# A list schedule that looks at all engines at once, with other tile counts and due times, in a chain of three kernels on one core

## The chip, the cores and the metric

The kernel runs on one core of a Trainium2 chip. The metric is the device time of one execution in microseconds, the median of a few runs. A profile of one execution shows what each engine did: TensorE (PE, with its weight loads as PEld), VectorE (DVE), ScalarE (ACT), GpSimd (POOL), and the queue of SyncE (SP), which issues all DMAs.

## The reference: what is computed

Three blocks follow one another, for a batch of 4:

```python
x  = attention(q_l, k_l, v_l, q_g, k_g, v_g)   # 8 heads of 64; 512 local positions with a
                                               # window of 32 to each side, 32 global positions
x  = moe(x, w_gate, wq, wk, wv, wo)            # 576 positions, 4 experts of causal attention (64 wide),
                                               # the best 2 of 4 by the gate, summed by their weights
h  = relu(x @ w_in)                            # 512 -> 1024
c  = conv over 3 neighbouring positions of h
y  = (h * sigmoid(c)) @ w_out                  # 1024 -> 512
```

`w_in`, `conv_w` and `w_out` arrive as 64-bit floats, and the kernel makes 32-bit floats of them (the "decode"). Every matrix product of the last two blocks is made of three products of high and low halves (`gh`/`gl`, `wuh`/`wul` and so on), each at one pass.

## The kernel before

All work of the program is recorded first and then put in order by a list schedule (`Recorder.schedule`). Each recorded piece has a due time, a number written by hand (`due(...)`, from the constants at the head: `PERIOD`, `A_AT`, `B_AT`, `FOLD`, `WOUT`, ...), a planned cost, and the tiles that it uses. The schedule walks through planned time and gives each engine that is free the ready piece with the lowest due time. A piece that begins a new tile is passed over while all buffers of that name are in use. The outcome is a fixed order of instructions on each engine; on the chip every engine takes its own in that order and waits where data or a buffer is not there yet. All engine calls are made on one line (308), so the rows of the profile are told apart by tile names.

The work of the program, by the functions that record it:

- `fold_gen`: 16 pieces of `w_in`, each loaded (256 KB), decoded by six DVE instructions and one of ACT, split into halves (`gl`; the low one by POOL) and multiplied with `wo` on PE into `wfh`/`wfl`. 16 pieces of `w_out` follow in `wout_gen`: the same decode, then `wuh` by ACT and `wul` by POOL. Columns 0 to 255 of `w_out` come first, then columns 256 to 511.
- `phase_a(b)`: the local and global attention in four chunks of two heads (`a0` to `a3` stand for the four batches below, `c0` to `c3` for the four chunks; tiles `raw`, `Pa`, `Pg`, `PA`, `vr`, `xh`, `xl`).
- `phase_b(b)`: the projections with `wqk` and `wv`, then 8 items of causal attention (scores `s<-kh,qh`, softmax in `w`, transposes, product with `vB`, result in `oh`/`ol`), and one for the last 32 rows.
- `phase_c(b)`: for two halves z of the positions, 8 times `s0` (PE `s<-oh,wfh`, ACT `hb` and `cv`), `s1` (two DVE `cv<-hb,cw,cv`, ACT), `s2` (DVE `cv<-cv,hb`, ACT `gh`, DVE `gl`), and then `project` (PE `s<-gh,wuh`, `s<-gl,wuh`, `s<-gh,wul`, in four column blocks m; m 0 and 1 need columns 0 to 255 of `w_out`, m 2 and 3 the rest).

The tile names that the change touches: `w2` (five buffers of 544 columns, for raw 64-bit weights, softmax rows and other weights alike), `d0`/`d1` (two buffers each, the decode's work tiles; `d` in the rows), `hb`/`cv` (three each). The decode of one piece on DVE is:

```python
dve.tensor_scalar(ai, up, 3, 0x3FFFFFF8, op0=ALU.logical_shift_left, op1=ALU.bitwise_and)
dve.scalar_tensor_tensor(di, up, -0x40000000, ai, op0=ALU.bitwise_and, op1=ALU.bitwise_or)
dve.tensor_scalar(ai, di, -0x800000, None, op0=ALU.bitwise_and)
dve.scalar_tensor_tensor(a, lo.bitcast(U32), 2.0 ** -52, a, op0=ALU.mult, op1=ALU.mult)
dve.tensor_tensor(d, d, a, op=ALU.add)
act.activation(a, up.bitcast(F32), AF.Abs)
dve.scalar_tensor_tensor(dst, a, GUARD, d, op0=ALU.is_ge, op1=ALU.mult)
```

Of the kernel before, what the change touches and what calls it, by code (L numbers as in the profile page):

```python
# [19 lines left out]
S = SL + SG  # L20
# [11 lines left out]
FIRST = [min(KEYS.index(n - 1), KEYS.index(n + 1) - 3) for n in range(NG_)]  # L32


PERIOD, A_AT, A_STEP, LOAD_AHEAD = 60.0, 0.0, 10.0, 20.0
B_AT, LAST, ITEMS, ITEM_STEP = 30.0, 34.0, 14.0, 2.5
C_AT, C_HALF, C_PROJ = 75.0, 25.0, 12.0
FOLD, FOLD_STEP, WOUT, WOUT_STEP = 30.0, 2.5, 75.0, 2.5


def local_mask():
# [110 lines left out]
class Recorder:  # L152
# [72 lines left out]
    def schedule(self):  # L225

        import heapq
        waits, after = {}, {}
        for n in self.nodes:
            waits[n] = len(n.deps)  # L230
            for d in n.deps:
                after.setdefault(d, []).append(n)
        used, left = {}, {}
        for n in self.nodes:
            for t in n.tiles:
                left[t] = left.get(t, 0) + 1
        last = {}
        ready = {}
        at = {}
        engines = []  # L240
        for n in self.nodes:
            if n.eng not in engines:
                engines.append(n.eng)
        free = {e: 0.0 for e in engines}
        ready = {e: [] for e in engines}
        for n in self.nodes:
            at[n] = 0.0
            if not waits[n]:
                ready[n.eng].append(n)
        times = [0.0]  # L250
        order, dma, now, back = [], 0.0, 0.0, []
        while len(order) < len(self.nodes):
            if not times:
                stuck = [(n.eng.name, n.due, n.calls[0][0], [t.name for t in n.new]) for e in engines for n in ready[e]]
                raise RuntimeError(f"no order: {stuck[:20]}")
            now = heapq.heappop(times)
            while times and times[0] <= now + 1e-9:
                heapq.heappop(times)
            for t0, t in [x for x in back if x[0] <= now + 1e-9]:
                used[t.name] -= 1  # L260
            back = [x for x in back if x[0] > now + 1e-9]
            lacking = set()
            for e in engines:
                if free[e] > now + 1e-9:
                    continue
                for n in sorted(ready[e], key=lambda n: (n.due, n.seq)):
                    if at[n] > now + 1e-9:
                        continue
                    need = {}
                    for t in n.new:  # L270
                        need[t.name] = need.get(t.name, 0) + 1
                    short = [k for k, c in need.items() if used.get(k, 0) + c > [t.bufs for t in n.new if t.name == k][0]]
                    if short or lacking & set(need):
                        lacking |= set(short)
                        continue
                    ready[e].remove(n)
                    for k, c in need.items():
                        used[k] = used.get(k, 0) + c
                    n.start = now
                    if e.name == "SP":  # L280
                        free[e] = now + 0.45
                        dma = max(dma, now + 0.5) + n.cost
                        n.end = dma + 1.6
                    else:
                        free[e] = n.end = now + n.cost
                    order.append(n)
                    heapq.heappush(times, free[e])
                    for m in after.get(n, ()):
                        at[m] = max(at[m], n.end + (0.02 if m.eng is e else n.lag))
                        waits[m] -= 1  # L290
                        if not waits[m]:
                            ready[m.eng].append(m)
                            heapq.heappush(times, at[m])
                    for t in n.tiles:
                        left[t] -= 1
                        last[t] = max(last.get(t, 0.0), n.end)
                        if not left[t]:
                            back.append((last[t] + 0.1, t))
                            heapq.heappush(times, last[t] + 0.1)
                    break  # L300
        return order

    def emit(self, tc):
# [75 lines left out]
def body(ctx, tc, kq, vA, w_gate, wqk, wv, woT, w_in, conv_w, w_out, cmask, out):  # L379
    nc = tc.nc  # L380
    NB = kq.shape[0]
    rec = Recorder()
    pe, act = rec.engine("PE", nc.tensor, cost_pe), rec.engine("ACT", nc.scalar, cost_act)
    dve, pool = rec.engine("DVE", nc.vector, cost_dve), rec.engine("POOL", nc.gpsimd, cost_pool)
# [5 lines left out]
    def T(shape, dt, name, bufs=1):  # L390
        return rec.tile(sb, shape, dt, name, bufs)
# [4 lines left out]
    def PS(*shape):  # L396
        return rec.tile(ps, [128] + list(shape), F32, "s", 5)
# [1 line left out]
    def PO(*shape):  # L399
        return rec.tile(ps, [128] + list(shape), F32, "t", 3)  # L400

    NW = 5

    def W2(dt=F32, n=512):
        w = T([128, S], F32, "w2", NW)[:, :n]
        return w if dt == F32 else w.bitcast(dt)

    def W1(name, dt=F32):
        w = T([128, 274], F32, name, 3)
        return w if dt == F32 else w.bitcast(dt)  # L410

    NG = 8
# [5 lines left out]
    def scale_pool(dst, src, s):  # L418
        pool.tensor_scalar(dst, src, s, 1.0, op0=ALU.mult, op1=ALU.mult)
# [240 lines left out]

    def consts_a():
        due(-15)
        w = W2()[:, :512]
        sp.dma_start(w, cmask[:, :512])
        dve.tensor_copy(lmask, w)

# [22 lines left out]
    def phase_b(b):  # L689
# [63 lines left out]
        for e in range(4):  # L753
            r0, p = 64 * (e % 2), e // 2
            for d, a in ((ql, qh), (qll, qlo)):
                act.activation(d[r0:r0 + 64, p, 32 * e:32 * e + 32], a[r0:r0 + 64, p, 512:544].bitcast(F32), AF.Copy)
        PL = W2(n=S)
        ms = T([128, 8], F32, "ms_last")
        tl = []
        for z in range(2):  # L760
            t = PS(512)
            n = 0
            if z == 0:
                rec.claim(PL)
            with rec.group():
              for p in range(2):
                for a, k in ((ql, kh), (ql, kl), (qll, kh)):
                    pe.matmul(t[:, :272], a[:, p], k[:, p, 272 * z:272 * z + 272], start=(n == 0),
                              stop=(n == 5 and z == 0))
                    n += 1  # L770
              if z:
                pe.matmul(t[:, 240:272], identb, last_mask, start=False, stop=True)
            dve.tensor_reduce(ms[:, z:z + 1], t[:, :272], axis=AX.X, op=ALU.max, negate=True)
            tl.append(t)
        dve.tensor_tensor(ms[:, 2:3], ms[:, 0:1], ms[:, 1:2], op=ALU.min)
        for z in range(2):
            act.activation(PL[:, 272 * z:272 * z + 272], tl[z][:, :272], AF.Exp, bias=ms[:, 2:3],
                           accum_out=ms[:, 4 + z:5 + z])
# [3 lines left out]
        scale_pool(PL, PL, ms[:, 7:8])  # L782
        PLT = T([128, 5, 128], F32, "PLT")
        t = PO(4, 128)
        rec.claim(PLT)
        with rec.group():
          for j in range(4):
            pe.transpose(t[:, j, :], PL[:, 128 * j:128 * j + 128], ident)
        act.activation(PLT[:, :4], t, AF.Copy)
        t = PO(4, 128)  # L790
        pe.transpose(t[:32, 0, :], PL[:, 512:544], ident)
# [223 lines left out]
```

## Time and profile before

| | us |
|---|---|
| median of 3 runs | 538.84 |
| lowest to highest | 538.46 to 539.15 |
| the profiled execution, its own time | 538.88 |
| its span, first to last instruction | 536.7 |
| PE busy | 480.3 |
| DVE busy | 372.1 |
| ACT busy | 316.6 |
| POOL busy | 127.5 |

The span is what the engines' rows cover; 2.2 us of the execution's own time lie outside of it. Busy PE time holds stretches in which the granted TensorE clock was at the lower of its two levels, so it is not the work at full clock. Shares over the whole span hide that the first third and the rest have different limits, so the rows further down are by stretches.

### The profile page before, as it was taken

What the parts mean: (1) busy time and instruction counts of PE and PEld (TensorE: products, weight loads), DVE (VectorE), ACT (ScalarE), POOL (GpSimd) and SP (SyncE); (2) the same over time, 40 slices, a digit from 0 to 9 for tenths busy, and PEclk for the clock granted to TensorE, in tenths of its full rate; (3) what the DMA queues carried; (4) which work ended last, traced back from release to release, by engine and by line L of the source; (5) the groups of instructions that cost most, each with busy time, mean ns of one, the idle gap of its engine ahead of it and who ended that gap; (6) DMA issues with size and microseconds to landing.
All of it is one profiled execution on the core that took longest, in us unless ns stands there. A gap on an engine that the chain in (4) does not pass through costs nothing.

```text
span 536.7 us, 14628 instructions
## 1 busy us (share of the span) xinstructions
PE 480.3 (89%) x5688; PEld 408.2 (76%) x5688; DVE 372.1 (69%) x1059; ACT 316.6 (59%) x1048; POOL 127.5 (24%) x222
## 2 busy tenths in 40 slices
PE   3777899977659999999999999999999999988997
PEld 1545689745445699997888799978888999767886
DVE  1789899989995846687567855556585646665760
ACT  1656574465555647765368875453796755536771
POOL 2234323244335330013322120131401201230000
PEclk9778999967666999999999999999999999999998
DMA  8475562435530100011015040000321000000001
GB/s 308 147 249 193 177 204 81 134 135 190 191 131 1 54 1 1 22 62 51 22 67 195 24 161 4 2 22 22 132 81 62 24 2 0 23 22 1 22 21 43
DMA packets 19045, 44.06 MB, mean 82 GB/s; under 512 B 2848, under 2 KB 8096, under 8 KB 18976
## 3 DMA queue, kind: packets, MB, share of 16 engines
q1 hardware_dynamic: 18976, 43.12, 23.8%
q8 instruction: 45, 0.74, 0.6%
q14 instruction: 24, 0.20, 0.1%
HBM read 38.66 MB, written 4.46 MB: 80 GB/s over the span
## 4 chain that ended last, share of the span: by engine, by line
PE 55%; DVE 11%; ACT 5%; issue 2%; POOL 0%; DVEq 0%; ACTq 0%; POOLq 0%
PE s L308 41%; PE t L308 13%; DVE cv L308 5%; DVE d L308 1%; ACT cv L308 1%; DVE gl L308 1%; ACT hb L308 1%; DVE PT L308 1%; DVE ml L308 1%; DVE stB L308 1%; ACT Pa L308 1%; ACT gh L308 0%; ACT PA L308 0%; ACT w L308 0%; POOL w L308 0%
## 5 line engine op out<-in xcount | busy, mean ns | idle before, releaser
L308 PE MATMUL s<-gh,wuh 128*128 128x272 f32 x256 | 79.1, 309 | 2.7 <-ACT gh L308 2.7
L308 DVE SCALAR_TENSOR_TENSOR cv<-hb,cw,cv 128x272 f32<-128x272 f32 x128 | 65.6, 524 | 22.3 <-ACT cv L308 19.3
L308 PE MATMUL s<-gl,wuh 128*128 128x272 f32 x256 | 75.3, 294 | 2.9 <-DVE gl L308 2.5
L308 PE MATMUL s<-gh,wul 128*128 128x272 f32 x256 | 74.5, 291 | 0.0
L308 POOL TENSOR_SCALAR w<-w,stB,gate 128x128 f32<-128x128 f32 (+3 forms) x64 | 40.3, 639 | 132.5 <-DVE stB L308 49.5
L308 PE MATMUL s<-raw 64*32 64x128 f32 (+2 forms) x1088 | 46.9, 329 | 13.3 <-DMA raw<-in_kq_dram 6.9
L308 PEld LDWEIGHTS s<-gh,wuh 128*128 128x128 f32 x256 | 49.0, 191 | 6.4 <-ACT gh L308 3.8
L308 PEld LDWEIGHTS s<-gl,wuh 128*128 128x128 f32 x256 | 49.0, 191 | 5.0 <-DVE gl L308 5.0
L308 POOL TENSOR_TENSOR Pa<-Pa,ml 128x512 f32<-128x512 f32 x32 | 36.2, 1147 | 67.0 <-DVE ml L308 33.7
L308 PEld LDWEIGHTS s<-gh,wul 128*128 128x128 f32 x256 | 48.9, 191 | 0.0
L308 PEld LDWEIGHTS s<-raw 64*32 64x32 f32 (+1 forms) x1088 | 24.9, 125 | 30.8 <-issue 12.7
L308 ACT ACTIVATE w<-s,stB 128x128 f32<-128x128 f32 (+3 forms) x64 | 33.3, 525 | 24.7 <-DVE stB L308 21.1
L308 ACT ACTIVATE Pa<-s,ml 128x128 f32<-128x128 f32 x128 | 45.1, 374 | 0.7 <-DVE ml L308 0.7
L308 PE MATMUL s<-oh,wfh 128*128 128x274 f32 x128 | 39.9, 312 | 0.2 <-ACT hb L308 0.2
L308 DVE TENSOR_REDUCE stB<-s 128x1 f32<-128x128 f32 (+3 forms) x64 | 29.4, 484 | 12.6 <-PE s L308 12.5
L308 DVE COPY PT<-t 128x128 f32<-128x128 f32 (+3 forms) x64 | 29.9, 486 | 11.5 <-PE t L308 11.0
L308 PE MATMUL s<-ol,wfh 128*128 128x274 f32 x128 | 37.8, 295 | 0.0
L308 PE MATMUL s<-oh,wfl 128*128 128x274 f32 x128 | 37.7, 294 | 0.0
L308 PE MATMUL s<-xh,wqkh 128*128 128x272 f32 x128 | 37.7, 294 | 0.0
L308 PE MATMUL s<-xh,wqkl 128*128 128x272 f32 x128 | 36.9, 289 | 0.0
L308 PE MATMUL s<-xl,wqkh 128*128 128x272 f32 x128 | 36.8, 288 | 0.0
L308 ACT ACTIVATE cv<-cv 128x272 f32<-128x272 f32 x64 | 27.5, 430 | 15.3 <-DVE cv L308 14.4
(140 smaller groups left out, 1301.6 us busy)
## 6 DMA issues: line engine op xcount, KB each, us to landing
vr<-in_vA_dram SPq DMA_DIRECT2D x32, 512.0 KB, 5.3
raw<-in_kq_dram SPq DMA_DIRECT2D x16, 672.0 KB, 4.1
out_dram<-y SPq DMA_DIRECT2D x32, 136.0 KB, 1.8
w<-in_w_in_dram SPq DMA_DIRECT2D x16, 256.0 KB, 3.4
w<-in_w_out_dram SPq DMA_DIRECT2D x16, 256.0 KB, 2.6
w<-in_wqk_dram SPq DMA_DIRECT2D x4, 256.0 KB, 6.6
w<-in_wv_dram SPq DMA_DIRECT2D x4, 128.0 KB, 2.0
w<-in_woT_dram SPq DMA_DIRECT2D x2, 256.0 KB, 2.8
```

Source lines behind the costliest of these rows:

```text
L308: getattr(n.eng.nc, method)(*map(real, args), **{k: real(v) for k, v in kw.items()})
```

## The change

`schedule` is rewritten: at each step of planned time the ready pieces of all engines are looked at in one list, by due time. The first piece in the list of each engine that is busy (`AHEAD = 1`) reserves its new tiles; when a tile name is short for a piece, all buffers of that name count as taken for the pieces behind it. Before, the engines were gone through one after the other, and only engines that were free.

The due times change a little (`FOLD` from 30 to 20.5 most). Raw 64-bit weights get two tiles of their own, `w64`; `w2` has four buffers of 512 columns; `hb` and `cv` have four buffers each and serve the decode too, in place of `d0`/`d1`. The decode's add goes from DVE to POOL. The score rows for the last 32 positions are cut at 512 and 32 columns in place of 272 and 272.

```diff
+AHEAD = 1
-PERIOD, A_AT, A_STEP, LOAD_AHEAD = 60.0, 0.0, 10.0, 20.0
-B_AT, LAST, ITEMS, ITEM_STEP = 30.0, 34.0, 14.0, 2.5
...
+FOLD, FOLD_STEP, WOUT, WOUT_STEP = 20.5, 2.5, 75.0, 2.5
...
-            lacking = set()
-            for e in engines:
-                if free[e] > now + 1e-9:
+            held, seen = dict(used), {}
+            for n in sorted((n for e in engines for n in ready[e] if at[n] <= now + 1e-9), key=lambda n: (n.due, n.seq)):
+                e = n.eng
+                busy = free[e] > now + 1e-9
+                if busy and seen.get(e, 0) >= AHEAD:
                     continue
...
+                short = [k for k, ts in need.items() if held.get(k, 0) + len(ts) > ts[0].bufs]
+                for k in short:
+                    held[k] = need[k][0].bufs
+                if short:
+                    continue
+                for k, ts in need.items():
+                    held[k] = held.get(k, 0) + len(ts)
+                if busy:
+                    seen[e] = seen.get(e, 0) + 1
+                    continue
...
-    NW = 5
-
-    def W2(dt=F32, n=512):
-        w = T([128, S], F32, "w2", NW)[:, :n]
-        return w if dt == F32 else w.bitcast(dt)
+    def W2():
+        return T([128, 512], F32, "w2", 4)
 
     def W1(name, dt=F32):
-        w = T([128, 274], F32, name, 3)
+        w = T([128, 274], F32, name, 4)
...
-        a, d = T([128, 256], F32, "d0", 2)[:, :w], T([128, 256], F32, "d1", 2)[:, :w]
+        a, d = W1("hb")[:, :w], W1("cv")[:, :w]
...
-        dve.tensor_tensor(d, d, a, op=ALU.add)
+        pool.tensor_tensor(d, d, a, op=ALU.add)
...
-        raw = W2(I32)
+        raw = T([128, 512], F32, "w64", 2).bitcast(I32)
...
-        PL = W2(n=S)
+        PL = W2(), T([128, 32], F32, "PL")
+        keys = slice(0, 512), slice(512, 544)
```

What stands where on the engines moves as follows. On PE, right behind the last product of `fold_gen` (`s<-gl,oh`) and one piece of scores, the order before goes on with the attention chunks of batch 1 (`raw`, `Pg`, `Pa`, `PGT`):

```order
L308 MATMUL s<-raw 32x128 x32
L308 MATMUL s<-raw 64x64
L308 MATMUL t<-ident,Pg 128x64 x6
L308 MATMUL s<-raw 64x480
L308 MATMUL s<-raw 64x64
L308 MATMUL t<-PGT,vr 64x32 x12
L308 MATMUL t<-ident,Pa 128x128 x8
```

In the order of the change the last product of `fold_gen` is followed by the items of batch 0's causal attention (`PT,vB`, `w`, `kh,qh`):

```order
L314 MATMUL s<-gl,ol 128x256
L314 MATMUL t<-PT,vB 64x128 x2
L314 MATMUL t<-ident,w_1522 128x128
L314 MATMUL t<-ident,w_1527 128x128
L314 MATMUL t<-PT,vB 64x128 x2
L314 MATMUL s<-kh,qh 128x256 x2
L314 MATMUL s<-kl,qh 128x256 x2
L314 MATMUL s<-kh,qlo 128x256 x2
```

So the causal attention of batch 0 stands ahead of three chunks of batch 1 and most of one of batch 2, behind which it stood before. `phase_c(0)` follows it, mixed with those chunks.

On DVE, near the last pieces of `w_out` (raw tiles `w_2030` to `w_2105`), the order before has decode steps (`d`) and steps of the local attention (`ml`) alone:

```order
L308 TENSOR_SCALAR d_2257<-d_2260 128x256
L308 TENSOR_TENSOR d_2254<-d_2254,d_2227 128x256
L308 SCALAR_TENSOR_TENSOR d_2257<-w_2085,d_2257 128x256
L308 TENSOR_SCALAR ml<-ml 128x4
L308 SCALAR_TENSOR_TENSOR d_2254<-d_2227,d_2254 128x256
L308 TENSOR_TENSOR d_2260<-d_2260,d_2257 128x256
L308 TENSOR_SCALAR d_2286<-w_2105 128x256
L308 TENSOR_REDUCE ml<-s 128x4
```

In the change, pieces of `w_out` (raw tiles `w_2354`, `w_2434`) stand between the convolution steps of `phase_c(0)` (128x272), with both in `hb` and `cv`:

```order
L314 TENSOR_TENSOR gl<-cv,gh 128x272
L314 SCALAR_TENSOR_TENSOR cv<-cv,hb 128x272
L314 SCALAR_TENSOR_TENSOR cv<-hb,cw,cv 128x272
L314 TENSOR_SCALAR hb<-w_2354 128x256
L314 TENSOR_TENSOR gl<-cv,gh 128x272
L314 SCALAR_TENSOR_TENSOR cv<-cv,hb 128x272
L314 SCALAR_TENSOR_TENSOR cv<-w_2354,hb 128x256
L314 TENSOR_SCALAR hb<-w_2434 128x256
L314 TENSOR_SCALAR hb<-cv 128x256
L314 TENSOR_TENSOR gl<-cv,gh 128x272
```

The decode no longer stands with chunks alone: the items and half of `phase_c(0)` have moved in beside it. The decode's add is gone from DVE. On POOL, at the first pieces of `w_out`, the change has it as `cv<-cv,hb`, between the scalings of the softmax rows (`w`) and the low halves (`wul`):

```order
L314 TENSOR_SCALAR w_1522<-w_1522,stB,gate 128x128
L314 TENSOR_SCALAR w_1527<-w_1527,stB,gate 128x128
L314 TENSOR_TENSOR cv<-cv,hb 128x256 x2
L314 TENSOR_TENSOR wul<-cv,wuh 128x256 x2
L314 TENSOR_TENSOR cv<-cv,hb 128x256
L314 TENSOR_SCALAR w_1657<-w_1657,stB,gate 128x256
```

Before, this place on POOL held `wul` and the scalings of the local attention alone; there are 32 such adds of 128x256 in the program. From the first `s0` of batch 1's `phase_c` on, both orders have the same pieces still to do, but for one score piece of 64 rows, which the change has done by then. Between the end of `fold_gen` and the last product of `project` for z = 0 of batch 0, the change has on PE what the order before has there, less these, which come later: four of the 13 groups of batch 1's projections, batch 1's first score piece, and in batch 2 the last transposes of chunk 0 and the first part of chunk 1.

## Rows read from the trace of the kernel before

**Rows 1.** The page's first part: busy time, share and instructions of each engine.

```profile
PE 480.3 (89%) x5688; PEld 408.2 (76%) x5688; DVE 372.1 (69%) x1059; ACT 316.6 (59%) x1048; POOL 127.5 (24%) x222
```

**Rows 2.** Busy time by stretches; last: granted clock, DMA share, GB/s.

```profile
27.00:104.90 77.90, 67.77 (x944) 56.52 (x942) 72.20 (x200) 46.47 (x166) 26.30 (x28) 0.93 0.52 169
104.90:156.80 51.90, 35.02 (x638) 24.81 (x634) 48.05 (x124) 28.63 (x106) 20.22 (x23) 0.70 0.53 181
156.80:203.40 46.60, 42.08 (x410) 31.81 (x409) 29.90 (x93) 26.20 (x105) 17.77 (x28) 0.86 0.05 16
203.40:233.40 30.00, 30.00 (x245) 29.67 (x244) 23.24 (x73) 21.75 (x59) 2.00 (x13) 1.00 0.03 11
233.40:281.50 48.10, 47.03 (x607) 39.67 (x606) 31.45 (x94) 27.70 (x94) 11.72 (x20) 1.00 0.16 56
281.50:384.70 103.20, 101.98 (x1225) 89.12 (x1223) 64.84 (x197) 64.25 (x215) 20.92 (x42) 1.00 0.22 73
384.70:486.80 102.10, 98.81 (x1133) 87.12 (x1132) 62.80 (x184) 61.77 (x198) 20.31 (x44) 1.00 0.08 28
486.80:536.70 49.90, 42.75 (x292) 40.01 (x289) 27.51 (x65) 28.57 (x73) 1.28 (x13) 0.93 0.07 23
```

**Rows 3.** PE in order of time: start, duration; end of a projection, and batch 1's phase_c.

```profile
233.22 0.29 PE L308 MATMUL s<-gh,wul 128*128 128x272 f32 x1
233.35 0.29 PE L308 MATMUL s<-oh,wfh 128*128 128x274 f32 x1
...
281.51 0.40 PE L308 MATMUL s<-oh,wfh 128*128 128x274 f32 x1
```

**Rows 4.** DVE groups by shape: busy us, mean ns, then idle before.

```profile
L308 DVE TENSOR_SCALAR d<-w 128x256 int32<-128x256 int32 x32 | 19.5, 618 | 1.8 <-DMA w<-in_w_in_dram 1.6
L308 DVE SCALAR_TENSOR_TENSOR d<-w,d 128x256 int32<-128x256 int32 x32 | 18.5, 579 | 0.6 <-POOL gl L308 0.3
L308 DVE SCALAR_TENSOR_TENSOR d<-d,d 128x256 f32<-128x256 f32 x32 | 16.6, 519 | 1.5 <-ACT d L308 1.1
L308 DVE SCALAR_TENSOR_TENSOR d<-w,d 128x256 f32<-128x256 uint32 x32 | 14.7, 459 | 0.6
L308 DVE TENSOR_TENSOR d<-d,d 128x256 f32<-128x256 f32 x32 | 14.2, 443 | 0.2
L308 DVE TENSOR_SCALAR d<-d 128x256 int32<-128x256 int32 x32 | 12.2, 382 | 0.3
```

**Rows 5.** DVE in order of time near 156 to 160 us: start, duration.

```profile
155.59 0.41 DVE L308 TENSOR_TENSOR d<-d,d 128x256 f32<-128x256 f32 x1
155.92 0.41 DVE L308 SCALAR_TENSOR_TENSOR d<-w,d 128x256 f32<-128x256 uint32 x1
...
156.55 0.42 DVE L308 SCALAR_TENSOR_TENSOR d<-d,d 128x256 f32<-128x256 f32 x1
...
157.23 0.29 DVE L308 TENSOR_SCALAR d<-w 128x256 int32<-128x256 int32 x1
...
158.43 0.41 DVE L308 SCALAR_TENSOR_TENSOR d<-w,d 128x256 int32<-128x256 int32 x1
...
158.88 0.29 DVE L308 TENSOR_SCALAR d<-d 128x256 int32<-128x256 int32 x1
...
159.67 0.83 DVE L308 TENSOR_TENSOR d<-d,d 128x256 f32<-128x256 f32 x1
```

**Rows 6.** POOL in order of time, the same stretch.

```profile
157.51 0.72 POOL L308 TENSOR_TENSOR wul<-d,wuh 128x256 fp32r<-128x256 f32 x1 [3.40 <-ACT wuh L308]
159.25 0.97 POOL L308 TENSOR_TENSOR wul<-d,wuh 128x256 fp32r<-128x256 f32 x1 [1.02 <-ACT wuh L308]
```

**Rows 7.** POOL groups over the whole span.

```profile
L308 POOL TENSOR_SCALAR w<-w,stB,gate 128x128 f32<-128x128 f32 (+3 forms) x64 | 40.3, 639 | 132.5 <-DVE stB L308 49.5 <-ACT cv L308 21.5 <-ACT PGT L308 21.0
...
L308 POOL TENSOR_TENSOR gl<-d,gl 128x256 fp32r<-128x256 f32 x16 | 12.7, 803 | 27.6 <-ACT gl L308 20.1 <-ACT gate L308 5.7 <-PE s L308 1.6
L308 POOL TENSOR_TENSOR wul<-d,wuh 128x256 fp32r<-128x256 f32 x16 | 12.3, 775 | 22.0 <-ACT wuh L308 22.0
```

**Rows 8.** Waits, over the whole span: us in total, times, longest.

```profile
DVE stB L308 <- PE s L308: 12.5, 20, 1.3
DVE PT L308 <- PE t L308: 11.0, 22, 1.6
```

More of the change, by code (lines that the diff above doesn't have):

```diff
@@ L32 @@
 FIRST = [min(KEYS.index(n - 1), KEYS.index(n + 1) - 3) for n in range(NG_)]
-PERIOD, A_AT, A_STEP, LOAD_AHEAD = 60.0, 0.0, 10.0, 20.0
-B_AT, LAST, ITEMS, ITEM_STEP = 30.0, 34.0, 14.0, 2.5
-C_AT, C_HALF, C_PROJ = 75.0, 25.0, 12.0
-FOLD, FOLD_STEP, WOUT, WOUT_STEP = 30.0, 2.5, 75.0, 2.5
+AHEAD = 1
+PERIOD, A_AT, A_STEP, LOAD_AHEAD = 60.0, -1.0, 10.0, 20.0
+B_AT, LAST, ITEMS, ITEM_STEP = 30.0, 35.0, 13.5, 2.4
+C_AT, C_HALF, C_PROJ = 75.0, 23.0, 11.0
+FOLD, FOLD_STEP, WOUT, WOUT_STEP = 20.5, 2.5, 75.0, 2.5
 def local_mask():
@@ L261, in schedule @@
             back = [x for x in back if x[0] > now + 1e-9]
-            lacking = set()
-            for e in engines:
-                if free[e] > now + 1e-9:
-                    continue
[L266 to L300, printed above, removed]
@@ new lines, in schedule @@
+            held, seen = dict(used), {}
[3 more added lines that the diff above has]
+                if busy and seen.get(e, 0) >= AHEAD:
+                    continue
+                need = {}
+                for t in n.new:
+                    need.setdefault(t.name, []).append(t)
+                short = [k for k, ts in need.items() if held.get(k, 0) + len(ts) > ts[0].bufs]
[8 more added lines that the diff above has]
+                    continue
+                for k, ts in need.items():
+                    used[k] = used.get(k, 0) + len(ts)
+                ready[e].remove(n)
+                n.start = now
+                if e.name == "SP":
+                    free[e] = now + 0.45
+                    dma = max(dma, now + 0.5) + n.cost
+                    n.end = dma + 1.6
+                else:
+                    free[e] = n.end = now + n.cost
+                order.append(n)
+                heapq.heappush(times, free[e])
+                for m in after.get(n, ()):
+                    at[m] = max(at[m], n.end + (0.02 if m.eng is e else n.lag))
+                    waits[m] -= 1
+                    if not waits[m]:
+                        ready[m.eng].append(m)
+                        heapq.heappush(times, at[m])
+                for t in n.tiles:
+                    left[t] -= 1
+                    last[t] = max(last.get(t, 0.0), n.end)
+                    if not left[t]:
+                        back.append((last[t] + 0.1, t))
+                        heapq.heappush(times, last[t] + 0.1)
@@ L662, in consts_a @@
         due(-15)
-        w = W2()[:, :512]
+        w = W2()
         sp.dma_start(w, cmask[:, :512])
@@ L760, in phase_b @@
         for z in range(2):
-            t = PS(512)
+            w = keys[z].stop - keys[z].start
+            t = PS(512)[:, :w]
             n = 0
-            if z == 0:
-                rec.claim(PL)
+            rec.claim(PL[z])
             with rec.group():
[L766 to L773, printed above, removed]
+                for p in range(2):
+                    for a, k in ((ql, kh), (ql, kl), (qll, kh)):
+                        pe.matmul(t, a[:, p], k[:, p, keys[z]], start=(n == 0), stop=(n == 5 and z == 0))
+                        n += 1
+                if z:
+                    pe.matmul(t, identb, last_mask, start=False, stop=True)
+            dve.tensor_reduce(ms[:, z:z + 1], t, axis=AX.X, op=ALU.max, negate=True)
             tl.append(t)
@@ L776, in phase_b @@
         for z in range(2):
-            act.activation(PL[:, 272 * z:272 * z + 272], tl[z][:, :272], AF.Exp, bias=ms[:, 2:3],
-                           accum_out=ms[:, 4 + z:5 + z])
+            act.activation(PL[z], tl[z], AF.Exp, bias=ms[:, 2:3], accum_out=ms[:, 4 + z:5 + z])
         dve.tensor_scalar(ms[:, 6:7], ms[:, 4:5], ms[:, 5:6], EPS, op0=ALU.add, op1=ALU.add)
@@ L781, in phase_b @@
         dve.tensor_tensor(ms[:, 7:8], ms[:, 6:7], glast, op=ALU.mult)
-        scale_pool(PL, PL, ms[:, 7:8])
+        for z in range(2):
+            scale_pool(PL[z], PL[z], ms[:, 7:8])
         PLT = T([128, 5, 128], F32, "PLT")
@@ L786, in phase_b @@
         with rec.group():
-          for j in range(4):
-            pe.transpose(t[:, j, :], PL[:, 128 * j:128 * j + 128], ident)
+            for j in range(4):
+                pe.transpose(t[:, j, :], PL[0][:, 128 * j:128 * j + 128], ident)
         act.activation(PLT[:, :4], t, AF.Copy)
         t = PO(4, 128)
-        pe.transpose(t[:32, 0, :], PL[:, 512:544], ident)
+        pe.transpose(t[:32, 0, :], PL[1], ident)
         act.activation(PLT[:32, 4], t[:32, 0], AF.Copy)
```

## The prediction

> **What bounds the kernel now.** I read the page's busy line first, then busy time by stretches cut where the program passes from one part to the next, then what DVE's decode steps take alone and beside POOL.
>
> The page says PE 89%, DVE 69% [rows 1], which reads like a PE-bound kernel. The stretches say otherwise [rows 2]. From 27.0 to 104.9 us (the fold and the chunks of batch 0) DVE is busy 72.20 of 77.9 us and from 104.9 to 156.8 (the w_out decode beside the chunks of batch 1) 48.05 of 51.9: 93% both times. PE is busy 35.02 of 51.9 in the second, at a mean granted clock of 0.70, so much of its busy time is the lower level. There DVE is the limit. From 203.4 on it turns: PE is busy 30.00 of 30.0, 47.03 of 48.1, 101.98 of 103.2 and 98.81 of 102.1 at clock 1.00, while DVE falls to 63% and 62% in the last two. Between, from 156.8 to 203.4, batch 0's causal attention runs with DVE busy 29.90 of 46.6. So DVE-heavy work and PE-heavy work stand one behind the other in the first half, and the second half is PE's. In the last stretch, 486.8 to 536.7, PE is busy 42.75 of 49.9: nothing is left to fill the waits of the last convolution.
>
> **The change, part by part.** Call F the end of the fold on PE, 104.9 us, and X the end of the projection for z = 0 in batch 0, 233.4 us [rows 3]. Call C the first product of batch 1's phase_c, 281.5 us [rows 3]. The order shows that the change has between F and X almost the work of before, but with causal attention and phase_c of batch 0 set beside the w_out decode, not behind it. So the question is how fast DVE can get through F to X, and whether PE keeps up.
>
> *DVE's work from F to X.* Before it is 48.05 + 29.90 + 23.24 = 101.2 us of busy time [rows 2], spread over 128.5 us. The change takes 16 of the 32 adds out of it: half of 14.2 us, 7.1 [rows 4]. The steps that go with the PE pieces moved behind X (reductions of one chunk, copies of a projection, of a kind that takes 0.16 to 0.7 us each) and with two first items moved ahead of F I put at 4 us, an estimate.
>
> *What the add costs on POOL, and DVE by it.* The rows have no such add on POOL; the nearest are its subtractions of the same shape, 803 and 775 ns [rows 7], so I take 0.79 us, 25 us for 32. POOL is busy 24% [rows 1], so it has the room. But DVE slows beside it. Alone the six decode steps on DVE take 0.29 + 0.41 + 0.29 + 0.41 + 0.41 + 0.42 = 2.23 us [rows 5]; their means over the program add up to 0.618 + 0.579 + 0.382 + 0.459 + 0.443 + 0.519 = 3.00 [rows 4]. One can be seen at it: the add at 159.67 takes 0.83 us, not 0.41 [rows 5], and a POOL subtraction runs from 159.25 to 160.22 [rows 6]. The excess is 0.77 us a piece, 24.6 us for 32, while POOL was busy 26.30 + 20.22 us [rows 2] and 0.72 + 0.97 up to the last piece [rows 6], 48.2 together: 0.51 us of DVE for a us of POOL. So an add saves DVE 0.44 us and costs it 0.79 x 0.51 = 0.40. The move to GpSimd is worth nothing to DVE, within 0.1 us a piece. From F to X that is +6.4 us for 16, and before F 16 adds leave (-7.1) and come back (+6.4): F is at 104.2, within 4 us. POOL's softmax scalings of the items (40.3 / 4 = 10.1 us a batch [rows 7]) now fall on a fuller DVE; I add 2 us, with 0 and 5 as bounds.
>
> The Trainium skill, in "SBUF — State Buffer", section "Who interferes with whom", says that a DVE instruction with two SBUF inputs, or in a two-port mode, and a GpSimd instruction that reads SBUF hold one shared pair of ports, and that the later one stands until the earlier has ended. The trace agrees with the direction (0.83 for 0.41 us), and by the mean it is half of that price. By the rule at its full length each add would cost DVE 0.79 us and save 0.44, so this part of the change would lose, and the sum below would come to 539 in place of 526.
>
> *X and C.* 101.2 - 7.1 - 4 + 6.4 + 2 = 98.5 us of DVE. At the 93% that DVE reaches where it is the limit [rows 2], that takes 105.9 us, so X comes at 104.2 + 105.9 = 210.1 in place of 233.4. From X to C PE was full, 48.1 us; now the pieces moved behind X are added. The four groups have 12 products each at 0.13 us from one start to the next [rows 3], 6.2 us; the rest I put at 60% of a chunk, with a chunk at (35.02 x 0.70) / 3.7 = 6.6 us of full clock [rows 2], 4.0 us. So C comes at 210.1 + 48.1 + 10.2 = 268.4, 13.1 us earlier.
>
> *Does PE keep up?* Its work from F to X at full clock is at most 35.02 x 0.70 + 42.08 x 0.86 + 30.0 = 90.7 us [rows 2], less 10: 81 in 106 us, a load of 0.76. In the first stretch a load of 67.77 x 0.93 / 77.9 = 0.81 went with a clock of 0.93 [rows 2]; at that clock 81 us of work take 87. It does, unless the clock stays low.
>
> *Behind C.* PE has 4.5 us of idle time from 281.5 to 486.8 and 7.2 from there to the end [rows 2]. The fourth buffer of hb and cv lets the last convolution run one step further ahead; I take 1 us of the 7.2, bounds 0 and 3. The two tiles for raw weights, four w2 in place of five (an item holds two, so two items are under way with either), and the cut at 512 and 32 columns I cost at nothing: their cover is PE's full stretches; if the rows of PE show gaps there, up to 4 us are lost. One POOL scaling becomes two, at most 0.4 us a batch, seen at the end of the last batch alone.
>
> The sum: 538.9 (the profiled execution, which is the median within 0.1) - 13.1 - 1 = 524.8; with 1 us for the last scaling and what the joints between the parts lose, 526.
>
> **The rivals.** *DVE waits inside the items (slower).* DVE takes its instructions as written, and each item has four places where it stands for another engine. From 156.8 to 203.4 it was idle 16.7 us with the items at hand [rows 2], and the waits for PE alone are 12.5 and 11.0 us over four batches [rows 8]. If all 16.7 come along into the decode stretch, X is at 227, C at 285.5, the end at 543. It decides from 13 us on. For it: PE's clock there may be low, so scores come late. Against: decode steps stand between the steps of an item in the order, and DVE, slowed by POOL, tends to be the late one.
>
> *The ports take their full price.* Each POOL us then costs DVE one, not 0.51: 0.39 us more for an add, 12.5 for 32, and about 1 us for the scalings. F moves by 6, X by 13: 539, no change. Against: the means of 32 pieces [rows 4], from which 0.51 comes. This is the rule of the Trainium skill, "SBUF — State Buffer", section "Who interferes with whom", with each add at its full length.
>
> *PE's clock stays low.* At 0.70, as in 104.9 to 156.8 [rows 2], 81 us of work take 116, X is at 220, the end at 535. For it: that stretch has decode and chunks, and half of the new stretch has too. Against: the load is 0.76, not 35.02 x 0.70 / 51.9 = 0.47.
>
> *Better.* DVE runs without gaps, 98.5 us in place of 105.9 (-7.4), and the fold, whose first loads now stand earlier in the SP queue, ends some us sooner: 513 to 518.
>
> **How the numbers follow.** My forecast as told, 519 to 533: 0.50. Better: 0.13. Low clock: 0.11. Full port price: 0.10. Waits in the items: 0.16. The likeliest gives 526. The range goes down to 513 and up to 541, which leaves out part of the slowest rival and a little below the best. A run tells 0.2% (1.1 us) from no change. Faster: 0.50 + 0.13 + 0.11 and 0.03 of the full price, 0.77. Same: 0.06. Slower: 0.17.
>
> **What would show it.** DVE busy 90% or more from the fold's end to the last piece of w_out, which then comes near 205 us; the end of batch 0's z = 0 projection at 210, and batch 1's first phase_c product near 269. From there to the end 254 us as before, within 3. Five decode steps on DVE with means that add up to 2.9 to 3.0 us without the add, if POOL costs what I take; 2.6, the five of today, if the adds cost nothing more. POOL adds near 0.79 us. PE's clock above 0.85 from 105 to 210. It would be wrong if DVE shows waits for PE, ACT or POOL of more than 13 us in that stretch, if F itself came later than 110, or if PE lost more than 5 us behind C because of the other tile counts.

## The result and the profile after

| | before | after |
|---|---|---|
| median, us | 538.79 (538.46 to 539.15, 4 runs) | 515.58 (512.06 to 516.68, 4 runs) |
| profiled execution, us (span) | 538.88 (536.7) | 516.68 (514.9) |

The ratio is 0.9558, with a 95% interval of 0.9512 to 0.9604: 23 us faster. The forecast was 526.0, 13 us faster, so the direction was right, the time was within the range, and the gain was nearly twice what was told.

The page's busy line of after answers to [rows 1]:

```profile
PE 468.6 (91%) x5688; PEld 400.2 (78%) x5688; DVE 359.1 (70%) x1026; ACT 313.5 (61%) x1048; POOL 155.5 (30%) x259
```

PE does as many matmuls, 5,688, in 11.7 us less busy time: less of it falls on the lower clock (the mean granted clock of the span is 0.936 before and 0.970 after). The other 10.1 of the 21.8 us by which the span is shorter were idle time of PE. DVE lost 33 instructions and 13.0 us, POOL gained 28.0.

Busy time by stretches of after, with the columns of [rows 2]. The cuts are the fold's end (109.9), the start of batch 0's phase_c (152.6), the end of its projection z = 0 (208.6), and the first product of phase_c of batches 1, 2 and 3:

```profile
27.00:109.90 82.90, 70.31 (x989) 59.19 (x979) 65.87 (x181) 46.80 (x171) 38.37 (x47) 0.92 0.47 151
109.90:152.60 42.70, 35.66 (x489) 24.39 (x489) 40.10 (x117) 27.14 (x102) 27.29 (x34) 0.96 0.30 103
152.60:208.60 56.00, 51.77 (x621) 46.67 (x620) 47.13 (x120) 41.70 (x137) 23.15 (x39) 0.94 0.30 102
208.60:268.40 59.80, 58.91 (x775) 49.19 (x773) 38.05 (x129) 35.60 (x124) 15.02 (x23) 1.00 0.23 74
268.40:369.90 101.50, 100.88 (x1221) 88.98 (x1220) 65.14 (x194) 64.02 (x216) 21.33 (x45) 1.00 0.19 62
369.90:471.00 101.10, 98.96 (x1133) 87.04 (x1132) 62.44 (x184) 59.29 (x194) 19.60 (x45) 1.00 0.09 30
471.00:514.90 43.90, 39.18 (x292) 36.91 (x289) 26.14 (x65) 27.71 (x73) 1.19 (x12) 0.99 0.08 27
```

Beside [rows 2], the last three stretches took 103.2, 102.1 and 49.9 us before; now they take 101.5, 101.1 and 43.9. The two cuts that the prediction calls X and C stand in PE's rows in order of time (start, duration), which answer to [rows 3]:

```profile
208.26 0.29 PE L314 MATMUL s<-gh,wul 128*128 128x272 f32 x1
...
268.37 0.39 PE L314 MATMUL s<-oh,wfh 128*128 128x274 f32 x1
```

X came at 208.6 (forecast 210.1, before 233.5) and C at 268.4 (forecast 268.4, before 281.5). So 13.1 us come from ahead of C, as told, and 8.7 from behind it, where 1 was told. All that lies ahead of C, before and after, in the columns of [rows 2]:

```profile
0.00:281.50 281.50, 236.79 (x3046) 191.95 (x3046) 216.99 (x613) 161.98 (x564) 84.96 (x124) 0.89 0.34 115
0.00:268.40 268.40, 229.62 (x3049) 187.27 (x3049) 205.33 (x583) 162.43 (x566) 113.42 (x159) 0.94 0.38 125
```

Of the 13.1 us, 7.2 are busy time of PE, at a mean granted clock of 0.94 and not 0.89, and 5.9 are its idle time.

The decode's DVE steps by shape, answering to [rows 4], and below them the add, which is now on POOL (there with one short form more):

```profile
L314 DVE SCALAR_TENSOR_TENSOR cv<-w,hb 128x256 int32<-128x256 int32 x32 | 19.2, 600 | 0.3
L314 DVE SCALAR_TENSOR_TENSOR cv<-hb,cv 128x256 f32<-128x256 f32 x32 | 17.0, 534 | 2.8 <-ACT hb L314 2.8
L314 DVE SCALAR_TENSOR_TENSOR hb<-w,hb 128x256 f32<-128x256 uint32 x32 | 16.1, 504 | 0.5
L314 DVE TENSOR_SCALAR hb<-w 128x256 int32<-128x256 int32 x32 | 13.6, 424 | 4.7 <-DMA w<-in_w_in_dram 4.5 <-DMA w<-in_w_out_dram 0.2
L314 DVE TENSOR_SCALAR hb<-cv 128x256 int32<-128x256 int32 x32 | 12.3, 384 | 0.3
...
L314 POOL TENSOR_TENSOR cv<-cv,hb 128x256 f32<-128x256 f32 (+1 forms) x33 | 26.0, 788 | 48.8 <-DVE hb L314 39.3 <-ACT Pa L314 4.8 <-DVE ml L314 2.8
```

The five means add up to 2.45 us; the same five were 2.56 before [rows 4], and 2.9 to 3.0 were told. The add takes 0.79 us on POOL, as told.

### The profile page after: what moved, and what is told of

Its sections match the earlier page's. It is cut to its first block, busy times and chain, and to the rows that moved or that the text cites. A ratio compares the mean times of both kernels' runs of the same rounds, so it can differ in the third digit from the quotient of the medians.

```text
span 514.9 us, 14575 instructions
## 1 busy us (share of the span) xinstructions
PE 468.6 (91%) x5688; PEld 400.2 (78%) x5688; DVE 359.1 (70%) x1026; ACT 313.5 (61%) x1048; POOL 155.5 (30%) x259
## 4 chain that ended last, share of the span: by engine, by line
PE 68%; DVE 16%; DMA 6%; ACT 5%; POOL 3%; issue 2%; SPq 0%; POOLq 0%; ACTq 0%; DVEq 0%
PE s L314 52%; PE t L314 16%; DVE cv L314 7%; DMA raw<-in_kq_dram 3%; DMA w<-in_w_in_dram 2%; DVE hb L314 2%; DVE gl L314 1%; DVE mg L314 1%; DVE stB L314 1%; DVE ml L314 1%; POOL w L314 1%; ACT hb L314 1%; POOL Pa L314 1%; ACT Pa L314 1%; DVE wqkl L314 1%
## 5 line engine op out<-in xcount | busy, mean ns | idle before, releaser
L314 POOL TENSOR_SCALAR w<-w,stB,gate 128x128 f32<-128x128 f32 (+3 forms) x64 | 41.5, 659 | 116.0 <-DVE gate L314 51.2
L314 POOL TENSOR_TENSOR Pa<-Pa,ml 128x512 f32<-128x512 f32 x32 | 37.3, 1183 | 46.4 <-DVE ml L314 24.8
L314 PE MATMUL s<-raw 64*32 64x128 f32 (+2 forms) x1088 | 43.7, 308 | 7.8 <-DMA raw<-in_kq_dram 6.7
L314 POOL TENSOR_TENSOR cv<-cv,hb 128x256 f32<-128x256 f32 (+1 forms) x33 | 26.0, 788 | 48.8 <-DVE hb L314 39.3
L314 PEld LDWEIGHTS s<-raw 64*32 64x32 f32 (+1 forms) x1088 | 22.9, 117 | 20.7 <-issue 11.1
```

The costliest lines, as they stand in the source:

```text
L314: getattr(n.eng.nc, method)(*map(real, args), **{k: real(v) for k, v in kw.items()})
```

## The experiments

All of them in one table. Ratios are to the kernel before on the same chip. X, C and the last convolution are read from PE's rows in order of time: "C to end" is from C to the end of the span, "last conv." from the first product of batch 3's phase_c to the end of the span, both from times rounded to a tenth. An early C is not all gain, because the orders differ in what stands ahead of it: in *tiles alone* and in *after, old table* 5.2 us less of PE's work stands there than in after, in *after, add on DVE* 6.6 us less, and in *after, three hb and cv* 4 to 5 us less (estimates, by the mean PE time of each kind of piece).

| kernel | median, us | ratio (95%) | X | C | C to end | last conv. |
|---|---|---|---|---|---|---|
| before | 538.8 | 1 | 233.5 | 281.5 | 255.2 | 49.9 |
| after | 515.58 | 0.9558 (0.9512 to 0.9604) | 208.6 | 268.4 | 246.5 | 43.9 |
| tiles alone | 518.52 | 0.9629 (0.9589 to 0.9669) | 200.1 | 259.4 | 256.3 | 43.9 |
| work tiles alone | 528.94 | 0.9822 (0.9782 to 0.9861) | 232.1 | 281.2 | 245.7 | 43.8 |
| schedule alone | 540.36 | 1.0028 (1.0004 to 1.0052) | 235.7 | 283.7 | 254.6 | 48.5 |
| table alone | 550.79 | 1.0228 (1.0200 to 1.0256) | 238.7 | 287.5 | 261.8 | 52.5 |
| add alone | 545.89 | 1.0142 (1.0085 to 1.0199) | 242.6 | 289.8 | 251.9 | 48.4 |
| add alone, order kept | 540.00 | 1.0029 (1.0006 to 1.0051) | 234.0 | 282.2 | 256.8 | 51.5 |
| after, three hb and cv | 529.74 | 0.9835 (0.9801 to 0.9869) | 201.1 | 266.0 | 263.6 | 50.0 |
| after, old schedule | 512.97 | 0.9534 (0.9506 to 0.9563) | 206.5 | 265.6 | 246.3 | 43.8 |
| after, old table | 519.83 | 0.9655 (0.9627 to 0.9684) | 202.4 | 259.3 | 257.1 | 43.8 |
| after, add on DVE | 526.88 | 0.9791 (0.9751 to 0.9830) | 207.9 | 268.3 | 259.1 | 43.9 |
| the same, order kept | 518.73 | 0.9637 (0.9611 to 0.9664) | 211.3 | 270.8 | 246.2 | 43.9 |
| after, POOL's add doubled | 530.70 | 0.9842 (0.9806 to 0.9877) | 224.0 | 283.1 | 246.5 | 43.9 |

**Which part moves batch 0's work forward.** *Tiles alone*, on the kernel before (with four `w2` of 512 columns and the cut of the last probabilities, which go with it):

```diff
-        w = T([128, 274], F32, name, 3)
+        w = T([128, 274], F32, name, 4)
...
-        a, d = T([128, 256], F32, "d0", 2)[:, :w], T([128, 256], F32, "d1", 2)[:, :w]
+        a, d = W1("hb")[:, :w], W1("cv")[:, :w]
...
-        raw = W2(I32)
+        raw = T([128, 512], F32, "w64", 2).bitcast(I32)
```

> The kernel before with the tile changes alone: raw weights in two tiles of their own, four w2 of 512 columns, the cut of the last probabilities at 512 and 32, decode's two work tiles taken from hb and cv with four buffers. The list schedule, the table of due times and the add on VectorE stay as before. The order already puts batch 0's attention and its phase_c beside the w_out decode. Theory A (a lack of work tiles held batch 0's attention behind the decode; tiles carry the gain): projection z = 0 of batch 0 ends near 210 us and not 233, the first product of batch 1's phase_c comes near 269, the time is 514 to 524. Theory B (the new table and the joint look at all engines carry it): 533 to 540. For the last convolution: if the fourth hb and cv buffer is what shortened it, first product of the last convolution to the end of the trace takes near 44 us as in the changed kernel; if that was chance of the clock, 50 as before.

It gives 20 of the 23 us by itself: tiles carry the gain, and the table and the schedule aren't needed for it. X (200.1) and C (259.4) come some 10 us earlier than was expected. That isn't more gain: 5.2 us of PE's work stand behind C in this order, and C to the end takes 256.3, 9.8 more than in after. *Work tiles alone* leaves the raw weights in `w2` and has only the first two of the three edits:

> The kernel before with one part of the tile changes: hb and cv have four buffers and decode takes its work tiles from them. Raw weights stay in w2 (five of 544 columns), and the schedule, the table, the add on VectorE and the cut of the last probabilities stay as before. In the order, batch 0's attention and phase_c stay behind the w_out decode. If the raw weights' own tiles carry the reorder and the fourth buffer the last convolution, then the projection z = 0 of batch 0 ends near 233 as before, batch 1's phase_c starts near 281, the last convolution's first product to the end takes 43 to 45 in place of 49.9, and the time is 529 to 534. If the four work tiles alone carry the whole gain: 514 to 521.

C stays at 281.2. So what brings the attention of batch 0 forward is that raw weights no longer take `w2`, of which each causal item needs two (with `w2` cut to four for it); the four work tiles alone don't do it. *After, three hb and cv*, further down, agrees: it has no fourth buffer, and X still comes at 201.1. What the count of `w2` and the cut of the last probabilities do by themselves was not tried apart. The four work tiles do the other half, all of it behind C. Busy time by stretches of this kernel, cut like the last three rows of after:

```profile
281.20:382.00 100.80, 100.63 (x1223) 88.80 (x1221) 66.39 (x197) 64.94 (x220) 22.97 (x45) 1.00 0.19 60
382.00:483.10 101.10, 98.28 (x1134) 87.27 (x1133) 61.64 (x184) 59.66 (x194) 17.85 (x44) 1.00 0.10 33
483.10:526.90 43.80, 39.13 (x290) 36.85 (x288) 26.14 (x65) 27.70 (x73) 1.20 (x12) 1.00 0.08 27
```

245.7 us from C to the end, as after has (246.5), with C where it was before. The two parts add up: 281.5 - 268.4 = 13.1 ahead of C, 255.2 - 245.7 = 9.5 behind it, 22.6 of 23.

**The fourth buffer, taken away.** *After, three hb and cv*:

```diff
-        w = T([128, 274], F32, name, 4)
+        w = T([128, 274], F32, name, 3)
```

> The changed kernel with three buffers of hb and cv in place of four. Batch 0's attention still stands beside the w_out decode in the order. If the fourth buffer shortened the last convolution, its first product to the end of the trace takes 48 to 50 us in place of 43.9 and the time is 519 to 523. If the 43.9 comes from the clock alone, it stays near 44 and the time near 516. If the fourth buffer matters for the decode, the projection z = 0 of batch 0 ends later than 212.

Its last two stretches:

```profile
379.80:479.60 99.80, 95.84 (x1057) 85.08 (x1052) 62.11 (x179) 58.63 (x188) 18.82 (x43) 1.00 0.09 29
479.60:529.60 50.00, 41.86 (x292) 38.70 (x288) 27.49 (x65) 28.59 (x73) 1.28 (x13) 0.95 0.07 24
```

The last convolution is back at 50.0. X comes at 201.1, so the fourth buffer isn't needed for the decode. The time, 529.7, is over 6 us above the 519 to 523 that were expected. With the longer convolution come waits of PE for `gh` and `gl`. First after's waits from 471 to 514.9 us, then this kernel's from 479.6 to 529.6 (total, times, longest):

```profile
PEld s L314 <- DVE gl L314: 2.1, 5, 0.5
...
PEld s L314 <- ACT gh L314: 1.3, 4, 0.6
```

```profile
PEld s L314 <- ACT gh L314: 4.6, 6, 1.5
...
PE s L314 <- ACT gh L314: 3.4, 5, 1.3
PEld s L314 <- DVE gl L314: 3.1, 8, 0.7
```

Of the 6.1 us, 50.00 - 41.86 - (43.90 - 39.18) = 3.4 are PE's idle time and 2.7 its busy time, at a mean clock of 0.95 and not 0.99. The table has this many times over: each of the eight kernels with four buffers ends in 43.8 or 43.9 us, each of the six with three in 48.4 to 52.5, whatever else was changed. In this stretch PE is idle 4.6 to 4.8 us with four buffers and 7.2 to 8.2 with three, and its mean clock is 0.99 to 1.00 with four and 0.89 to 0.96 with three. Its busy time there is 39.1 to 39.2 us with four and 41.2 to 44.8 with three, but busy time times clock is 39.5 to 39.9 in all six with three, so the lower clock accounts for nearly all of the longer busy time. The rest of this kernel's loss lies between C and the last convolution (213.6 us, 202.6 in after), 4 to 5 us of it as work that stands ahead of C in after.

**Schedule and table.** *Schedule alone* puts the joint look over all engines and the held tiles into the kernel before, *after, old schedule* takes them out of after. *Table alone* and *after, old table* do that with the constants:

```diff
-            lacking = set()
-            for e in engines:
-                if free[e] > now + 1e-9:
+            held, seen = dict(used), {}
+            for n in sorted((n for e in engines for n in ready[e] if at[n] <= now + 1e-9), key=lambda n: (n.due, n.seq)):
...
-FOLD, FOLD_STEP, WOUT, WOUT_STEP = 30.0, 2.5, 75.0, 2.5
+FOLD, FOLD_STEP, WOUT, WOUT_STEP = 20.5, 2.5, 75.0, 2.5
```

> The kernel before with the new list schedule alone (one look over all engines, tiles kept for work due first). Tiles, due times and the add stay as before. Theory A (tiles carry the gain): the order moves the items of batch 0 forward a little but leaves its phase_c where it was, so the time is 535 to 541. Theory B: 515 to 526, since the schedule is what brings the attention forward.

> The changed kernel with the list schedule of before; tiles, table and add stay changed. Its order differs from the changed kernel's at a few ties only. Theory A (tiles carry the gain; the joint look does nothing here): 513 to 518. Theory B (the schedule carries it): 525 or more.

> The kernel before with the new table of due times alone. Theory A (tiles carry the gain): order hardly moves in batch 0, time 534 to 541. Theory B (table and schedule carry it): 515 to 530.

> The changed kernel with the due times of before. The new table alone made the kernel before 12 us slower. If it costs the same with the new tiles: 503 to 511. If it only moves work across batch 1's phase_c here (5.2 us less of PE work stands ahead of it with the old table) and PE is full behind it: 513 to 519, with the first product of batch 1's phase_c near 263. If table and tiles need each other: 522 or more.

The new schedule gave no gain: 1.5 us slower alone, and without it after is at 512.97, an interval that overlaps with that of after. The table is another matter. Alone it costs 12 us, which neither theory had. With the new tiles it is worth 4 to 5 us (by the medians, and by 0.9655 against 0.9558), although C comes at 259.3 without it. What stands ahead of C is 5.2 us less there (by the mean PE time of each kind of piece), and behind C 257.1 - 246.5 = 10.6 us are given back, so 5.4 are lost among the later batches. Where, was not tried apart. So the table pays only with the tiles, and by less than the expectation asked for. No kernel here beats after by more than the runs can tell.

**The add on GpSimd.** *Add alone* is the one line of the change, *after, add on DVE* its reverse:

```diff
-        dve.tensor_tensor(d, d, a, op=ALU.add)
+        pool.tensor_tensor(d, d, a, op=ALU.add)
```

> The kernel before with decode's add on GpSimd alone. By the prediction a us of GpSimd costs VectorE 0.51 us, so the move is worth nothing: 537 to 541. Relief (GpSimd beside VectorE costs nothing more): VectorE loses 33 adds of 0.44 us, 14.5 us, in stretches in which it was busy 93%, so up to 15 us less: 523 to 530. Full price (each GpSimd us costs VectorE one): 33 times 0.35 us more, 12 us: 549 to 552. Means of the five steps left on VectorE: 2.9 to 3.0, 2.4 to 2.6, and above 3.2 in turn.

> The changed kernel with decode's add back on VectorE; everything else stays changed. By the prediction's price (0.51 us of VectorE for each us of GpSimd) nothing changes: 514 to 518. Relief (the add on GpSimd costs VectorE nothing more): VectorE gets 33 adds of about 0.4 us back, 14 us at 80 to 90% busy: 526 to 532. Relief that is hidden, because VectorE no longer sets the end in these stretches: under 519 with VectorE fuller.

Two answers that contradict each other: 7 us slower to move it (545.89, in none of the three ranges expected), 11 us slower to move it back. In both kernels the list schedule placed everything anew. So the same two edits were made at the point where instructions are issued, behind the schedule, with all else in its order. This is the edit of before; in after the last line has `nc.vector`:

```diff
-                    getattr(n.eng.nc, method)(*map(real, args), **{k: real(v) for k, v in kw.items()})
+                    getattr(getattr(n, 'at_emit', n.eng.nc), method)(*map(real, args), **{k: real(v) for k, v in kw.items()})
...
+        rec.nodes[-1].at_emit = nc.gpsimd
```

> The kernel before with decode's add issued on GpSimd and every other instruction in the order of before (the earlier run with the add alone moved let the list schedule place everything anew and was 7 us slower). If the other order made it slower: 533 to 540. If the move itself does, because decode has two buffers of each of its work tiles there and GpSimd holds them longer: 542 to 549, with VectorE waiting for GpSimd or ScalarE at d from 105 to 157 us.

> The changed kernel with decode's add issued on VectorE in place of GpSimd, and every other instruction on every engine in the changed kernel's order (the earlier run with the add back on VectorE let the list schedule place everything anew, and it put 6.6 us less of PE work ahead of batch 1's phase_c). If GpSimd's add relieves VectorE where VectorE is the limit: 521 to 530, with batch 1's first phase_c product at 274 to 282. If the earlier 11 us came from the other order alone: 514 to 518.

With the order kept, the add on POOL costs 1 to 2 us in before (1.0029) and gains 3 to 4 in after (518.73 against 515.58, 0.9637 against 0.9558). The other 6 and 8 us belonged to the order alone. The 518.73 lies between the two cases that were expected. The busy line of the kernel with after's order and the add on DVE, then of the one in which POOL does a second add:

```profile
PE 474.2 (92%) x5688; PEld 403.4 (78%) x5688; DVE 361.8 (70%) x1059; ACT 313.3 (61%) x1048; POOL 129.7 (25%) x226
```

```diff
                     getattr(n.eng.nc, method)(*map(real, args), **{k: real(v) for k, v in kw.items()})
+                    if getattr(n, 'twice', None):
+                        n.eng.nc.tensor_tensor(real(args[2]), real(args[0]), real(args[2]), op=ALU.add)
...
+        rec.nodes[-1].twice = True
```

> The changed kernel with a second GpSimd addition of the same shape behind each of decode's adds (its result goes to the work tile that ScalarE writes next and is used by nothing), every other instruction in the changed kernel's order. GpSimd has 26 us more in the decode. Prediction's price, 0.51 us of VectorE for one of GpSimd: 13 us more of VectorE in stretches where it is busy 79 to 88%, so 522 to 529, and the five steps' means rise by 0.4 us from 2.45. Full price: 26 us more, 533 to 541. No price: 514 to 518, with the means at 2.45.

```profile
PE 479.3 (91%) x5688; PEld 407.7 (77%) x5688; DVE 368.3 (70%) x1026; ACT 312.9 (59%) x1048; POOL 179.7 (34%) x292
```

From these the price of a POOL us for DVE can be read: without its adds (14.2 us at 446 ns each) DVE is at 347.6 in the first; after has 359.1 with 25.8 us more of POOL, so 11.5 / 25.8 = 0.45; the doubled add has 9.2 more for 24.2, so 0.38. The same for the kernel before with the add on POOL, its order kept:

```profile
PE 479.0 (89%) x5688; PEld 407.4 (76%) x5688; DVE 365.8 (68%) x1026; ACT 317.1 (59%) x1048; POOL 151.2 (28%) x255
```

(365.8 - 372.1 + 14.2) / (151.2 - 127.5) = 0.33, with [rows 1]. So 0.33 to 0.45 us, from one profile of each kernel, where 0.51 was told. The Trainium skill, "SBUF — State Buffer", section "Who interferes with whom", says that a GpSimd instruction that reads SBUF and a VectorE instruction with two SBUF inputs, or in a two-port mode, shut each other out for the whole instruction. These runs agree in the direction. The price that the prediction worked out from this rule, 1 for 1, is more than double what they show.

The doubled add cost 15 us all the same, a little above the 522 to 529 that a price of 0.51 gave. But the price wasn't 0.51: DVE's busy time rose by 9.2 us and not 13, and the five means by 0.21 us and not 0.4. So more than DVE's busy time is in the 15 us. ScalarE's waits in this kernel, then those in after, both over the whole span:

```profile
ACT hb L314 <- POOL hb L316: 33.3, 21, 4.6
```

```profile
ACT hb L314 <- POOL cv L314: 14.2, 13, 2.5
```

The chain of one piece (DVE, POOL, ACT, DVE) gets longer. The end of the fold went from 109.9 to 119.9, and F to X from 98.7 to 104.1. How the 15 us divide between DVE's busy time and the chain stays open.

## Why the prediction was right, and where its size was off

*X and C* came at 208.6 and 268.4, told 210.1 and 268.4, and *tiles alone* against *work tiles alone* shows the mechanism: with raw weights in their own tiles the items stand beside the decode. But the terms of that sum were off, and cancelled: F came 5.7 us late, F to X took 98.7 us and not 105.9, and X to C 59.8 and not 58.3. That C fits to a tenth is luck.

**The DVE work** from 27 us to X was put at 72.20 - 7.1 + 6.4 ahead of F and 98.5 behind it, 170 in all; it is 65.87 + 40.10 + 47.13 = 153.1. The add has little part in it: with it back on DVE and the order kept, the same work is 155.6. The prediction took the decode's steps at the means of before [rows 4]; in after's order they cost less, as the six show in the kernel that keeps this order with the add on DVE:

```profile
L314 DVE SCALAR_TENSOR_TENSOR cv<-w,hb 128x256 int32<-128x256 int32 x32 | 17.1, 534 | 0.8
L314 DVE SCALAR_TENSOR_TENSOR hb<-w,hb 128x256 f32<-128x256 uint32 x32 | 16.1, 505 | 0.5
L314 DVE SCALAR_TENSOR_TENSOR cv<-hb,cv 128x256 f32<-128x256 f32 x32 | 15.4, 485 | 1.4 <-ACT hb L314 1.1
L314 DVE TENSOR_TENSOR cv<-cv,hb 128x256 f32<-128x256 f32 x32 | 14.2, 446 | 0.2
L314 DVE TENSOR_SCALAR hb<-w 128x256 int32<-128x256 int32 x32 | 13.0, 406 | 3.4 <-DMA w<-in_w_in_dram 2.5 <-DMA w<-in_w_out_dram 0.9
L314 DVE TENSOR_SCALAR hb<-cv 128x256 int32<-128x256 int32 x32 | 9.9, 310 | 0.3
```

They add up to 2.69 us, to 3.00 before, and 32 times that difference is 10 us. Order alone moves them: *after, add on DVE* has the same tiles and engines as this kernel in another order, and its six add up to 2.93. Another 2.0 us of DVE's work had been done ahead of 27 us. **DVE's fullness** from F to X was put at 93%. It is 87.23 / 98.7 = 88%, and 91% up to the last piece of `w_out`, as the sign asked. Ahead of F, where the prediction left DVE as full as before, it is 65.87 / 82.9 = 79%.

**F** was put at 104.2, within 4 us, and came at 109.9. Here the prediction read before 1.4 us late: the fold's last product, in before and in after, stands here:

```profile
103.19 0.28 PE L308 MATMUL s<-gl,ol 128*128 128x256 f32 x1
...
109.64 0.28 PE L314 MATMUL s<-gl,ol 128*128 128x256 f32 x1
```

So the fold ended at 103.5 before, and 6.4 us later after. The new order has only some 1.4 us more of PE's work ahead of this product (an estimate, by the time from start to start of each kind of product). Two stretches of before up to there, then two of after:

```profile
27.00:80.00 53.00, 43.73 (x691) 34.20 (x688) 48.68 (x124) 33.59 (x128) 18.28 (x19) 0.90 0.63 208
80.00:103.50 23.50, 22.82 (x251) 22.04 (x250) 22.11 (x72) 11.86 (x37) 7.40 (x8) 1.00 0.24 79
```

```profile
27.00:80.00 53.00, 40.41 (x676) 30.27 (x667) 42.60 (x102) 30.97 (x120) 24.36 (x28) 0.88 0.57 183
80.00:109.90 29.90, 29.90 (x315) 28.92 (x313) 23.27 (x80) 15.83 (x51) 14.01 (x20) 0.99 0.31 96
```

PE is full for the last 30 us ahead of F, but it nearly was in before too. The delay comes from ahead of 80 us, where DVE and PE both have more gaps than before. The last loads of `w_in` are issued later (start of the first, time to the end of the last; before, then after):

```profile
69.43 10.87 SPq L308 DMA_DIRECT2D w<-in_w_in_dram  x4
...
79.23 16.12 SPq L314 DMA_DIRECT2D w<-in_w_in_dram  x5
```

The prediction put the cost of the two tiles for raw weights at nothing, and in its case "better" it had the fold's loads earlier. These tiles may be what holds these loads back: the kernels with them end the fold at 106.5 to 109.9 us (119.9 with the doubled add), those without at 103.1 to 107.2. This was not tried apart.

*The add is worth nothing to DVE, within 0.1 us a piece*: 361.8 - 359.1 = 2.7 us over 32 pieces, 0.08. Right, with the price at 0.45 in place of 0.51. The 0.51 laid to POOL all that the steps take beyond their lone times, but that changes with the order at the same POOL work (2.93 and 2.69 above, with POOL busy 129.3 and 129.7 us). The sign that was to show it (five means of 2.9 to 3.0) was badly chosen, because those means shift with the order: in after's order the five add up to 2.24 with the add on DVE, and the add on POOL raises them to 2.45.

*Behind C only 1 us, bounds 0 and 3*: this is the term that was mis-sized. Measured: 8.7, and 9.5 in *work tiles alone*; C to the end took 246.5, where the sign asked for 254 within 3. 6.0 of the 8.7 lie in the last convolution. The prediction looked at its 7.2 us of idle time as what could be won and took one. It left out that PE's busy time there was itself stretched by a lower clock (0.93, [rows 2]): 42.75 us, now 39.18. In before the clock falls right behind such a wait; three us with PE busy 1.87, and the next three:

```profile
489.80:492.80 3.00, 1.87 (x13) 1.45 (x12) 2.96 (x9) 2.26 (x6) 0.20 (x2) 1.00 0.00 0
492.80:495.80 3.00, 2.88 (x17) 2.66 (x16) 2.40 (x7) 2.63 (x7) 0.10 (x1) 0.74 0.00 0
```

Not every wait is followed by this: in *after, three hb and cv* PE is busy 1.27 of the 3 us from 491.6, and the clock stays at 1.00. The fourth buffer took idle time and lower clock together: 2.4 us of idle time and 3.6 of busy time. The other 2.7 came out of the two stretches before, which the prediction had called full; why is open.

The rivals: DVE's idle time from F to X is 11.5 us, under the 13 from which the waits decide. F at 109.9 stayed just under the 110 that would have shown the prediction wrong. The clock is 0.96 and 0.94, so it doesn't stay low. The full port price is ruled out by 0.33 to 0.45. Two sums of the rivals are off by less than 1 us, which changes no chance: with the waits C would be at 285.1, and with the low clock the end at 536. The time fell into the range of "better", but by neither of its reasons: DVE has gaps, and the fold ends later. PE lost nothing behind C by the other tile counts, and the last piece of `w_out` left DVE at 205.2, as told.

## What to carry to other kernels

Ask of each tile name who else takes its buffers: raw weights that shared `w2` with the attention held a whole part of the program back, and four buffers of `hb` and `cv`, shared by decode and convolution, in place of three and two more for the decode, were worth 10 us. Where a tail has waits, look at its granted clock and count the busy time at the lower clock as well as the idle time: here both went. And where a list schedule decides, one edit moves everything: test it once with the order kept, or 6 to 8 us of other order are taken for its effect.

## What the runs showed of the hardware

A us of GpSimd, spent on adds of 128x256, raised VectorE's busy time by 0.33 to 0.45 us in three pairs of kernels of one order. The mean of one and the same decode step, 128x256 from the raw weights, went from 364 ns (*tiles alone*) over 424 (after) to 618 [rows 4], so means of VectorE steps are no constants to carry from one order into another. That the engines beside it decide this fits the price above, but was not tried apart. The length of the last convolution repeated to 0.1 us in all eight kernels with four buffers, at a granted clock of 0.99 to 1.00; with three buffers it varied from 48.4 to 52.5 us, at 0.96 to 0.89.
